# Transposes shared out anew between TensorE and DMA in a planned attention-and-experts kernel

## The chip, the cores and the metric

One core of one Trainium2 chip runs the whole program. The metric is the device time of one execution in microseconds (us). Three runs before the change took 315.46, 314.18 and 314.10 us; their median is 314.18.

## What is computed

The reference is an attention with soft-capped scores, whose output goes through four attention experts of which each token uses two. `B, H, S, Dh = 8, 12, 448, 64`; the model width `D` is 768, there are `E = 4` experts with one head of 64.

```python
scores = cap * tanh((q @ k.T) / sqrt(64) / cap)           # 8 x 12 heads of 448 x 448, cap = 30
x = softmax(scores) @ v                                    # heads side by side: 8 x 448 x 768
logits = x @ w_gate                                        # 4 experts, the best 2 of each token
w = softmax over the 2 chosen logits
for e in range(4):
    a = softmax(causal(x @ wq[e] @ (x @ wk[e]).T / 8))     # 448 x 448, each row sees its past
    out += (e chosen) * w * (a @ (x @ wv[e]) @ wo[e])
```

The soft cap bounds the first scores, so no row maximum is needed there.

## The kernel before

**Two stages, interleaved.** The work of the first stage goes by pairs of heads: 48 pairs, six for each batch (`HP = 6`). The last batch's pairs (42 to 47) hold only their first 320 queries (`W1`); the remaining 128 queries of its six pairs are packed into two more items, 48 and 49. For an item the keys of two heads are cast to 16 bits on GpSimd (POOL), turned by TensorE (PE) with four transposes (three of 128 keys, one for the 64-key tails of both heads), the query likewise, and one VectorE (DVE) copy brings both into `qk`. Scores are computed transposed (keys on partitions) into the banks `X` (three: the first key block of both heads, and the tails of both) and `Y` (two, used twice: `Y1`, `Y2`). ScalarE (ACT) applies tanh to X, Y1 and Y2 and then one exp to all seven slots of the item (lines L768 and L780). The value product gives outputs and, from a column of ones, the sums; DVE divides (L823, L826) into `xk`, PE turns `xk` (L841) and DVE copies it to `xT` (L850).

**Second stage, batch by batch.** When a batch's six pairs are done, `b_v` computes logits and values of all experts, POOL works out the gate (ranks, two one-hot masks `ms`, weights `mw`), `b_mask` widens each of the two masks to the 128 columns of a pair of experts (`mB`) and turns it by a DMA transpose into `mT`, `b_qk` computes keys and queries, and the query is multiplied with the turned mask as it leaves PSUM (`qm`, L951). So one score matmul handles four experts at once, each token with its own expert. `b_score` puts a slot's 1024 score columns into X0 and X1, ACT applies exp (L1066), POOL zeroes what lies ahead of the diagonal (L1076, L1083), `b_pv` makes the product with the values, `b_ot` adds the two slots on POOL (`oS`, L1141) and turns the sum by DMA into `oT`, and `b_wo` multiplies with `wo` and stores four windows of rows. The slots of batch b run beside pairs `6(b+1)+5` and `6(b+1)+6`, those of batch 6 beside items 48 and 49 (`exps`, L756). The last batch has no later pairs to hide behind: `last` and `last2` compute it by themselves at the end. There the causal mask is put into PSUM by matmuls with an identity (`negm`, L1290) before the scores are added.

**The order is planned.** Every operation is noted in a graph with the engine, an estimated duration and what it reads and writes. Exps and tanhs of ACT have a fixed order; they give due times, and `solve` (L130) plays the program through, engine by engine, taking the operation due first among those ready, with some seeded noise (`SEEDS`, `JIT`). Operations marked `first` go ahead of others when they come ready soon. The result is one order for each engine; on the chip each engine takes its instructions in that order and waits for what they need. DMA loads, stores and transposes are issued by SyncE (SP), also in the planned order. Three PSUM banks (`A0` to `A2`) serve everything but the scores while the pairs run; the five score banks are lent out only at the end.

**Lines that matter later.** `turned` (L387) issues a DMA transpose; `cast` (L615) the POOL casts (L620 keys, L635 key tails `ktz`, L639 values); `tr` (L647) the transposes of an item; `tr_first_tails` (L685) those of pair 0's tails, which are done apart; `fill` (L729) the score matmuls (L717 heads, L727 tails). `fill` groups an item's Y2 with the next item's X into one operation unless the item is in the set `alone` (L757), which holds the items that the second stage uses X0 and X1 beside. `normed` (L1189) ends the last batch's rows: division, transpose (L1208), the copy `oTL`, the product with `wo` (L1223), copies into `ob` and stores. The tiles `ob` are those into which `b_wo` writes as well. `evac` lets the planner choose DVE or ACT for a copy from PSUM, after ACT's fixed list is over (L377 in the profile, whatever engine).

## Time and profile before

| what | value |
|---|---|
| median of three runs | 314.18 us |
| the profiled execution | 314.04 us, of which 312.0 us from first to last instruction (the span) |
| mean granted TensorE clock | 0.983 |
| moved by DMA | 53.29 MB, 171 GB/s over the span |
| HBM read, written | 36.19 MB, 11.01 MB |
| instructions | 8950 |

The page of the profile gives busy time of each engine, the span in 40 slices, the chain of work that ended last, and the costliest groups of instructions by line of the kernel. Views of the trace give the same for any stretch: instructions in order of time with what ended the idle time before them ("[1.46 <-PE X L727]" is 1.46 us of idle time that ended when that matmul was done), busy time by stretch, waits by cause, DMA issues. In a busy-time row the engines stand as busy us and, in brackets, the number of instructions; then come the granted TensorE clock, the share of time in which the 16 DMA engines moved data, and GB/s. PE's matmuls are pipelined, so their durations overlap. In the 40 slices of 7.8 us the DMA share falls through the run:

```profile
DMA  6899999869976995789873698855014200531136
GB/s 183 182 227 221 297 272 253 220 168 268 251 189 159 313 272 159 187 179 255 217 164 78 201 310 196 129 162 154 2 41 146 97 2 19 87 120 60 36 148 207
```

### The profile page before, as it was taken

The numbers are of one execution on the slowest core, as the hardware profiler recorded it, in microseconds if no ns is written. First come the engines' busy times: TensorE is split into PE (matmuls) and PEld (weight loads), VectorE is DVE, ScalarE is ACT, GpSimd is POOL, SyncE is SP. The second block draws the span as 40 slices with busy tenths as digits, with TensorE's granted clock in tenths as the row PEclk, the third lists the DMA queues.
The fourth block names the chain that finished last, engine by engine and source line by source line (L and its number), as shares of the span: only waits on it lengthen the run. The fifth ranks groups of instructions, "written<-read, shape, count | busy, mean of one in ns | idle before, by whom it ended". The sixth has DMA issues, their size and how long they took to land.

```text
span 312.0 us, 8950 instructions
## 1 busy us (share of the span) xinstructions
PE 280.9 (90%) x3476; PEld 190.4 (61%) x3476; DVE 217.8 (70%) x645; ACT 291.8 (94%) x246; POOL 181.4 (58%) x498
## 2 busy tenths in 40 slices
PE   7677689979898899989998999999999989999993
PEld 3354356658564766657655776568664866667761
DVE  2345556666764886869766877788776877786883
ACT  4699999998999999999999999999999999999562
POOL 7694436996787452984785576947866414701200
PEclk9979979998999999999999999999999999999999
DMA  6899999869976995789873698855014200531136
GB/s 183 182 227 221 297 272 253 220 168 268 251 189 159 313 272 159 187 179 255 217 164 78 201 310 196 129 162 154 2 41 146 97 2 19 87 120 60 36 148 207
DMA packets 87482, 53.29 MB, mean 171 GB/s; under 512 B 48144, under 2 KB 83728, under 8 KB 87440
## 3 DMA queue, kind: packets, MB, share of 16 engines
q1 hardware_dynamic: 87136, 52.49, 65.5%
q8 instruction: 27, 0.44, 0.6%
q10 hardware_dynamic: 304, 0.23, 0.2%
q14 instruction: 15, 0.12, 0.2%
HBM read 36.19 MB, written 11.01 MB: 151 GB/s over the span
## 4 chain that ended last, share of the span: by engine, by line
ACT 66%; PE 20%; DMA 4%; POOL 3%; issue 3%; DVE 2%; SPq 1%; ACTq 0%; POOLq 0%
ACT yp L768 34%; ACT yp L780 28%; ACT pB L1066 4%; PE A L1164 2%; DMA kf<-in_k_dram 2%; PE Y L717 2%; PE A L937 2%; PE A L910 2%; PE A L802 2%; DMA out_dram<-ob 2%; PE X L1057 1%; PE A L1116 1%; PE A L663 1%; PE A L795 1%; PE X L727 1%
## 5 line engine op out<-in xcount | busy, mean ns | idle before, releaser
L780 ACT ACTIVATE yp<-yp 128x3136 f16<-128x3136 f16 (+4 forms) x51 | 139.0, 2726 | 0.0
L768 ACT ACTIVATE yp<-Y 128x896 f16<-128x896 f32 (+2 forms) x100 | 94.6, 946 | 2.6 <-PE Y L717 2.6
L768 ACT ACTIVATE yp<-X 128x1344 f16<-128x1344 f32 (+2 forms) x50 | 65.1, 1302 | 2.5 <-PE X L727 1.5
L802 PE MATMUL A<-v,yp 128*128 128x65 f16 x1116 | 56.4, 194 | 0.0
L802 PEld LDWEIGHTS <-yp 128*128 128x128 f16 x1116 | 49.0, 98 | 5.7 <-issue 2.9
L795 PE MATMUL A<-vtz,yp 128*128 128x130 f16 x186 | 41.3, 222 | 7.9 <-ACT yp L780 3.7
L826 DVE TENSOR_TENSOR xk<-A,rca 128x256 f16<-128x256 f32 (+1 forms) x96 | 39.7, 415 | 2.9
L717 PE MATMUL Y<-qk 64*128 64x448 f16 (+2 forms) x216 | 36.2, 341 | 5.7 <-ACT yp L768 5.1
L639 POOL CAST v<-vf 128x384 f16<-128x384 f32 x48 | 24.6, 514 | 27.0 <-PE A L802 22.1
L620 POOL CAST k<-kf 128x384 f16<-128x384 f32 x47 | 23.7, 513 | 24.2 <-PE A L663 15.0
L683 DVE COPY qk<-A 128x960 f16<-128x960 f16 x47 | 29.5, 650 | 6.1 <-PE A L653 6.0
L377 DVE COPY ob<-A 128x384 f32<-128x384 f32 (+1 forms) x56 | 30.4, 554 | 4.7 <-PE A L1164 2.9
L823 DVE RECIPROCAL rca<-A 128x4 f32<-128x4 f32 (+1 forms) x96 | 17.1, 178 | 21.0 <-PE A L802 19.4
L795 PEld LDWEIGHTS <-yp 128*128 128x128 f16 x186 | 18.1, 97 | 19.7 <-ACT yp L780 9.3
L623 POOL CAST q<-qf 112x512 f16<-112x512 f32 x44 | 27.2, 619 | 2.3 <-DMA qf<-in_q_dram 2.1
L717 PEld LDWEIGHTS <-qk 64*128 64x128 f16 x324 | 15.0, 93 | 21.7 <-issue 15.5
L1164 PE MATMUL A<-wo,oT 128*128 128x384 f16 x112 | 26.2, 326 | 1.4 <-DVE xT L850 0.5
L1131 DVE SCALAR_TENSOR_TENSOR oB<-A,rcb,mw 128x256 f16<-128x256 f32 x54 | 25.5, 481 | 1.8
L850 DVE COPY xT<-A 128x448 f16<-128x448 f16 (+1 forms) x48 | 18.0, 376 | 9.9 <-PE A L841 9.5
L1141 POOL TENSOR_TENSOR oS<-oB,oB 128x512 f16<-128x512 f16 x14 | 16.1, 1154 | 14.5 <-DVE oB L1131 8.7
L1116 PE MATMUL A<-vB,pB 128*128 128x260 f16 x133 | 22.2, 275 | 1.6 <-DVE oB L1131 1.2
L653 PE MATMUL A<-ident,q 112*128 112x112 f16 x192 | 22.5, 219 | 0.0
(210 smaller groups left out, 569.8 us busy)
## 6 DMA issues: line engine op xcount, KB each, us to landing
qf<-in_q_dram SPq DMA_DIRECT2D x23, 448.0 KB, 6.0
kf<-in_k_dram SPq DMA_DIRECT2D x23, 384.0 KB, 5.2
vf<-in_v_dram SPq DMA_DIRECT2D x23, 384.0 KB, 4.9
out_dram<-ob SPq DMA_DIRECT2D x23, 384.0 KB, 3.8
out_dram<-ob SPq DMA_DIRECT2D x9, 192.0 KB, 2.9
ktf<-in_k_dram SPq DMA_DIRECT2D x46, 32.0 KB, 4.9
vtf<-in_v_dram SPq DMA_DIRECT2D x46, 32.0 KB, 4.3
ob<-in_moe_wv_dram SPq DMA_DIRECT2D x2, 384.0 KB, 4.1
```

What stands on the lines that cost most here:

```text
L377: (nc.scalar.copy if o.eng == "ACT" else nc.vector.tensor_copy)(dst(), src())
L623: e(q16[i], qf[s][:, h].rearrange("p h (c d) -> p c h d", c=QC))
L683: lambda: nc.vector.tensor_copy(qk[t], bank16(g)[:, 0 : S + 512]),
L717: nc.tensor.matmul(dst[:, g, o], t[r, S + 128 * (c + 1) : S + 128 * (c + 2)], t[r, qs], start=True, stop=True,)
L768: ACTS[what, p] = act(c_act(n * (b - a)), lambda: nc.scalar.activation(y[:, a:b, 0:n], src[:, 0 : b - a, 0:n], AF.Tanh, scale=isc / capf), ...
L780: act(c_act(n * (b - a), False), lambda a=a, b=b, n=n: nc.scalar.activation(y[:, a:b, 0:n], y[:, a:b, 0:n], AF.Exp, scale=capf), ks, ks, f ...
L795: nc.tensor.matmul(ps[:, n, :, :], y[:, 2, w : w + 128], vtz[u], start=(n == 0), stop=False, skip_group_check=True,)
L802: nc.tensor.matmul(ps[:, n, h, :], y[:, SLOT[c][h], w : w + 128], v16[u][:, h, c, :], start=False, stop=(c == 2), skip_group_check=True,)
L826: dve(c_dve(128 * m), lambda g=g, i=i, rc=rc, m=m: nc.vector.tensor_tensor(xk[p % NXK][:, 2 * i : 2 * i + m, :, :], view(g)[:, 0:m, :, 0:D ...
L1116: nc.tensor.matmul(bank(g)[:, 0 : E * (Dh + 1)], pB[pi][:, o : o + 128], vB[x][:, c, :, :], start=(t == 0), stop=(t == len(cs) - 1),)
L1131: dve(c_dve(E * Dh) + 0.06, lambda g=g, k_=k_, n=n: nc.vector.scalar_tensor_tensor(oB[s][:, n, :, :], view(g)[:, :, 0:Dh], rcb[k_][:, 0, : ...
L1164: nc.tensor.matmul(bank(g)[:, 0 : D // 2], oT[x][n // 2][:, r, n % 2, :], wo2[r][:, c0:c1], start=(r == 0), stop=(r == 1),)
```

## The change

1. **Masks and outputs of batches 0 to 3** (`b < MD`, `MD = 4`). The masks `mB` are turned by TensorE: eight transposes a slot, and `qm` is now the product of a query kept in `qB` (a new copy from PSUM, two a batch) with the turned mask in PSUM. The query product no longer waits for the masks, and `b_qk` is noted after the gate. The slot sums `oS` are turned by eight TensorE transposes, with two copies to `oT`. Batches 4 to 6 keep the DMA transposes.
2. **Keys from pair 34 on** (`KD = 34`). Keys and tails of two pairs are cast by POOL into `kz` and turned by one DMA transpose of eight blocks into `kd` (three buffers of two pairs), from which the score matmuls read. TensorE turns only the query; the copy into `qk` is that of the query alone.
3. **x from pair 36 on** (`NAT = 36`). The query copy puts the queries into natural order, so `xk` needs no permutation and is turned by a DMA transpose straight into `xT`; the last pair of each batch (41 and 47) stays on TensorE. The value product then reads windows that run 64 columns past an item's last slot, into a pad.
4. **The last batch's causal masks** for the first 320 queries: the `negm` matmuls are gone; POOL zeroes the blocks after the exp. The masks of the last 128 queries (`neg2`) stay as they are.
5. **The start.** The key tails' cast is marked `first`, and POOL takes operations of that kind early (before 12 us of the plan). Item 0 is in `alone`, so its Y2 is filled without item 1's X. A wait for the first Y is dropped from pair 0's tail transpose. The first exp on ACT, which loads the table, waits for `ident` as well.
6. **The end.** Batch 6's first slot runs beside item 47 instead of 48. `b_wo` of batch 6 does three windows; its last 64 rows are put beside the 64 new rows of the last batch's third window by a POOL copy, and share its product with `wo`. `normed` writes its rows into the tiles `kf`, which held the keys, instead of `ob`, and has three tiles `oTL` instead of two.
7. **The planner's numbers**: estimates of DMA times, rank constants, due times, seeds. They change the order of instructions throughout.

The core of the diff:

```diff
-LAND = 2.2
+LAND = 1.95
-JIT = 0.784
-TWIRE = 0.2
-TOCC = 0.18
+JIT = 0.549
+TWIRE = 0.1
+HEAD = 12.0
+MD = 4
+NAT = 36
+KD = 34
...
-                if e in ("PE", "DVE") and not o.first:
+                early = e == "POOL" and t < HEAD
+                if (e in ("PE", "DVE") or early) and not o.first:
                     for t2, u in c:
-                        if u.first and u.due + lag < t + o.occ + 0.0 and t2 < t + max(SWITCH + 0.01, min(o.occ, 0.25)):
+                        if u.first and u.due + lag < t + o.occ + 0.04 and t2 < t + (
+                                o.occ if early else max(SWITCH + 0.01, min(o.occ, 0.25))):
...
+        def kcast(p):
+            s, o, x, j = p // 2 % NST, p % 2, p % (2 * NST), p // 2
+            dst = kz[j % 2][:, o]
+            gp(0.45, lambda: nc.gpsimd.tensor_copy(
+                dst[:, 128:].rearrange("p (c h d) -> p c h d", h=2, d=Dh),
+                kf[s][:, 2 * o : 2 * o + 2].rearrange("p h (c d) -> p c h d", c=KC)),
+                [("kf", x)], [("kz", j % 2, o, "k")], name=f"k16_{p}")
+            gp(0.2, lambda: nc.gpsimd.tensor_copy(
+                dst[:, 0:128], ktf[s][:, o].rearrange("p g d -> p (g d)")),
+                [("ktf", x, 0), ("ktf", x, 1), ("zk", s)], [("kz", j % 2, o, "t")],
+                name=f"kt16_{p}")
...
+        elif p % 2 == 0:
+            kcast(p)
+            kcast(p + 1)
+            j = p // 2
+            turned(8, lambda: kd[j % 3].rearrange("p o c -> p (o c)"),
+                   lambda: kz[j % 2].rearrange("p o c -> p (o c)"),
+                   [("kz", j % 2, o_, y) for o_ in range(2) for y in "kt"], [("kd", j % 3)],
+                   f"kT{p}")
...
-    exps = {HP * (b + 1) + (XOFF if b < LB - 1 else (6, 7))[s]: (b, s) for b in range(LB) for s in range(2)}
-    alone = set(exps)
+    late = {6: (5, 7)}
+    exps = {HP * (b + 1) + o: (b, s) for b in range(LB) for s, o in enumerate(late.get(b, XOFF))}
+    alone = {0, *exps}
...
+        if p >= NAT and p not in (PB - 1, NP - 1):
+            turned(nb, lambda: xT[b % 2][:, j, 0 : 128 * nb],
+                   lambda: xk[p % NXK][:, 0:nb].rearrange("p n g d -> p (n g d)"),
+                   [("xk", p % NXK, 0), ("xk", p % NXK, 1)], [("xT", b % 2, j)], f"xT{p}",
+                   due=due)
+            return
...
+                if b < MD:
+                    dve(c_dve(S), lambda g=g, r=r: nc.vector.tensor_copy(
+                        qB[x][r], bank(g)[:, 0:S]), [("q", b, r)], [("qB", x, r)], g, name=f"qB{b}")
+                    continue
...
+        if b < MD:
+            for r in range(2):
+                g = Group(AUX + XB, 1.3)
+
+                def mm(g=g, r=r):
+                    for n in range(4):
+                        nc.tensor.transpose(
+                            bank16(g)[:, 128 * n : 128 * (n + 1)],
+                            mB[s][:, r, n].rearrange("p e d -> p (e d)"), ident)
+
+                pe(0, mm, [("mB", s), "ident"], [("mt", b, s, r)], g, occ=0.22, name=f"mT{b}")
+                dve(c_dve(S, True), lambda g=g, r=r: nc.vector.tensor_tensor(
+                    qm[s][r], qB[x][r], bank16(g)[:, TL:512], ALU.mult),
+                    [("mt", b, s, r), ("qB", x, r)], [("qm", s, r)], g, name=f"qm{b}")
+            return
...
-        for n in range(4):
+        for n in range(4 if b < LB - 1 else 3):
...
-        o = ob[n]
+        o, u = kf[n].rearrange("p h x -> p (h x)"), n % 3
+        kk = [("kf", 2 * n), ("kf", 2 * n + 1)]
...
+        if n == 2:
+            y = (LB - 1) % 2
+            gp(0.25, lambda: nc.gpsimd.tensor_copy(oTL[u][:, :, 0:64], oT[y][:, 1, :, 1, 64:128]),
+               [("oT", y, 1)], [("oTL", u, 1)], name="oT6")
+            ko.append(("oTL", u, 1))
...
-            for e in (1, 0):
-                n = 128 if part == 0 else W1
-                pe(n, lambda e=e, n=n: nc.tensor.matmul(
-                    bank(g2[e])[:, 0:n], ident, negm[:, 0:n], start=True, stop=False,
-                    skip_group_check=True), ["negm", "ident", ("kB", x, r)],
-                    [("sL", r, part, e)], g2[e], name="mk")
+            pe(0, lambda: None, [("kB", x, r)], [("sL", r, part, 1)], g2[1], occ=0.0, name="op")
...
+            for o, base in ((64 + W1 * part, 0), (64 + W1 + 192, -64))[0 : 1 + part]:
+                def below(o=o, base=base):
+                    blk = pP[r][:, :, o : o + 128]
+                    nc.gpsimd.affine_select(
+                        out=blk, in_=blk, compare_op=ALU.is_ge, fill=0.0, base=base,
+                        pattern=[[0, 2], [1, 128]], channel_multiplier=-1)
+
+                gp(0.38, below, [], [("pB", pi, part) for pi in (2 * r, 2 * r + 1)], name="diagL")
...
-        o.first = o.name[:2] in ("sX", "sY", "sT", "tr", "qk", "k1", "q1", "ge")
+        o.first = o.name[:2] in ("sX", "sY", "sT", "tr", "qk", "k1", "q1", "ge", "kt")
```

177 lines of the change are left out of this document (111 added, 66 removed).

## Prediction

> **What bounds the kernel now.** I read the page's first part, then busy time by stretch, then what ScalarE (ACT) waited for.
>
> ```profile
> span 312.0 us, 8950 instructions
> PE 280.9 (90%) x3476; PEld 190.4 (61%) x3476; DVE 217.8 (70%) x645; ACT 291.8 (94%) x246; POOL 181.4 (58%) x498
> ```
>
> The profiled execution took 314.04 us, 2.04 more than its span; the median of the three runs is 314.18. I work on the span and add 2.04 at the end. ACT is busy for 94%. The stretches tell where the rest lies:
>
> ```profile
> core 0: us, PE busy (x) PEld busy (x) DVE busy (x) ACT busy (x) POOL busy (x), PEclk, DMA share, GB/s
> 0.00:12.51 12.51, 8.63 (x71) 4.68 (x72) 3.58 (x12) 5.61 (x8) 8.80 (x48) 1.00 0.81 196
> 12.51:66.00 53.49, 45.14 (x525) 28.11 (x525) 28.94 (x83) 53.49 (x39) 35.56 (x110) 0.94 0.96 237
> 66.00:190.00 124.00, 114.26 (x1442) 79.33 (x1442) 93.07 (x267) 122.84 (x93) 83.58 (x212) 0.99 0.80 208
> 190.00:276.00 86.00, 82.25 (x1032) 56.30 (x1030) 66.20 (x193) 85.99 (x71) 49.68 (x124) 1.00 0.39 92
> 276.00:290.04 14.04, 13.49 (x224) 10.81 (x220) 11.06 (x40) 13.38 (x13) 1.53 (x4) 1.00 0.29 100
> 290.04:312.00 21.96, 17.13 (x194) 11.17 (x189) 14.90 (x54) 10.51 (x27) 2.26 (x2) 0.99 0.42 139
> ```
>
> From 12.51 to 290.04 ACT runs almost without a break. That stretch is 277.53 us of tanh and exp, which the change doesn't touch. TensorE (PE) is nearly as full late in it: 82.25 of 86.00 us from 190 to 276. DMA goes the other way, from a share of 0.96 to 0.39. Two stretches are not ACT's: the first 12.51 us, with 5.61 of ACT work, and the last 21.96, with 10.51. ACT's waits by cause, within the stream:
>
> ```profile
> ACT yp L768 <- PE Y L717: 2.6, 2, 1.7
> ACT yp L768 <- PE X L727: 1.5, 1, 1.5
> ACT yp L768 <- PE X L717: 0.9, 1, 0.9
> ACT pB L1066 <- PE X L1057: 0.7, 1, 0.7
> ```
>
> The 1.5 and the longest of the first row (1.7) lie before 12.51. What can be had between 12.51 and 290.04 is the other two, 0.9 + 0.7 = 1.6 us, however much work moves there. So this is a change of the two ends; in the middle it can chiefly do harm.
>
> **The start.** The timeline of the first 13 us, with the issues of that stretch:
>
> ```profile
> 1.22 1.19 ACTq L481 DMA_DIRECT2D ktf<-in_k_dram  x2
> 6.23 0.92 ACT L768 ACTIVATE yp<-Y 128x896 f16<-128x896 f32 x1 [0.91 <-PE Y L717]
> 7.32 0.53 POOL L635 CAST ktz<-ktf 128x128 f16<-128x128 f32 x2
> 8.34 0.66 DVE L683 COPY qk<-A 128x960 f16<-128x960 f16 x1 [0.19 <-PE A L653]
> 8.61 1.29 ACT L768 ACTIVATE yp<-X 128x1344 f16<-128x1344 f32 x1 [1.46 <-PE X L727]
> 10.91 0.34 PE L663 MATMUL A<-ident,k 128*128 128x128 f16 x3 [1.66 <-POOL k L620]
> 11.59 0.92 ACT L768 ACTIVATE yp<-Y 128x896 f16<-128x896 f32 x1 [1.69 <-PE Y L717]
> 11.89 0.77 DVE L623 CAST q<-qf 112x512 f16<-112x512 f32 x2 [2.89 <-DMA qf<-in_q_dram]
> 17.07 0.93 ACT L768 ACTIVATE yp<-Y 128x896 f16<-128x896 f32 x1
> ktf<-in_k_dram ACTq DMA_DIRECT2D x2, 16.0 KB, 3.4
> ```
>
> Pair 0's X tanh waits 1.46 us for the scores of the key tails. Their cast stands at 7.32 on GpSimd (POOL), behind memsets, though the tails were issued from 1.22 on and landed 3.4 us later: the second, issued near 1.8, by about 5.3. From cast to tanh the trace needs 8.61 − 7.32 = 1.29 us. Cast at once, the scores stand at 5.3 + 1.29 = 6.6, before the Y tanh ends at 6.23 + 0.92 = 7.15. So the first wait, 1.46, goes.
>
> The second wait, 1.69, is an order: pair 0's second Y half is filled by one PE instruction group together with pair 1's X, and that stands behind the transposes of pair 2's keys, which start at 10.91 after waiting for a late load. With pair 0 in `alone` the Y half is filled for itself and needs only bank Y, free at 7.15. That wait goes too: 3.15 together.
>
> What is late next: pair 1's X needs its copy, which ends at 8.34 + 0.66 = 9.00; the new tanh would want it at 12.51 − 3.15 = 9.36, with 0.36 of matmul between: just met. Then pair 1's last Y is filled with pair 2's X, whose q is cast at 11.89 when it lands. Cast 0.4, transposes 0.4, copy 0.66 and two score matmuls 0.6, with hand-overs, end near 14.2; ACT would want it 3.15 before its present 17.07, at 13.9. I take **−2.8**; ends −1.2 (pair 2's q lands 1.6 late, as much as the keys made PE wait) and −3.15.
>
> **The middle.** What is moved:
>
> ```profile
> L841 PE MATMUL A<-perm,xk 128*128 128x128 f16 x144 | 16.3, 223 | 1.1 <-DVE xk L826 0.9
> L947 DVE CAST kB<-A 128x448 f16<-128x448 f32 x14 | 8.7, 624 | 8.1 <-PE A L937 7.9
> L850 DVE COPY xT<-A 128x448 f16<-128x448 f16 (+1 forms) x48 | 18.0, 376 | 9.9 <-PE A L841 9.5
> L389 SPq DMA_TRANSPOSE mT<-mB x14: 1232/1258/2520, 60.1 to 269.4; - x14
> mT<-mB SPq DMA_TRANSPOSE x14, 2.8
> SPq L389 <- POOL oS L1141: 41.4, 5, 14.0
> 202.23 0.63 DVE L683 COPY qk<-A 128x960 f16<-128x960 f16 x1
> 215.03 1.29 ACT L768 ACTIVATE yp<-X 128x1344 f16<-128x1344 f32 x1
> ```
>
> A 128 by 128 transpose occupies PE for 16.3 / 144 = 0.113 us. Batches 0 to 3 gain 16 for the masks and 8 for the outputs each: 24 × 0.113 = 2.7 us a batch, 10.9 in all, before about 190 us. VectorE (DVE) gains per batch two q evacuations like `kB` (0.62) and two output copies (about 0.38): 2.0 us, 8.0 in all. Off PE come four key transposes for each of 14 pairs (34 to 47) and 35 x transposes (five pairs of four, five of three): 91 × 0.113 = 10.3 us, nearly all after 190. DVE loses ten x copies, 3.8 us; its key and query copy shrinks.
>
> Early there is room: PE idles 8.35 us from 12.51 to 66 and 9.74 from 66 to 190, DVE 24.6 and 30.9. With 18 us of idle for 10.9 of new work, and ACT never idle beside it, I cost this at nothing; without that cover up to half of 2.7 us a batch would stand before the batch's scores.
>
> On SP eight mask and eight output transposes of about 1.25 us leave; seven key transposes (two pairs, eight blocks each) and ten x transposes come. A key transpose is issued in 1.26 us and lands 2.8 after its issue, and waits for POOL casts that exist now. It has time: the copy of pair 36's keys starts at 202.23 and their tanh at 215.03, 12.8 us of lead. Last pairs of a batch keep TensorE, so x's DMA latency isn't on a batch's path. The new waits stand in SP's queue, ahead of stores and the last loads; those lead by whole pairs. The Trainium skill (VectorE: DVE Perf Modes, "The three transpose paths") gives 390 ns a block on TensorE and 1309 ns by DMA and prefers TensorE where PSUM can take the result; by it, an estimate, a key transpose would take 10.5 us and seven of them 73. The trace disagrees, with 2.8 us for the same eight blocks. I take **0** for the middle; ends −1.6 (both waits gone) and +3 (half of 2.7 us in two batches).
>
> **The end.** After the stream:
>
> ```profile
> 289.16 0.88 ACT L780 ACTIVATE yp<-yp 128x768 f16<-128x768 f16 x1
> 290.00:300.00 10.00, 10.00 (x117) 7.03 (x114) 7.94 (x33) 5.62 (x17) 2.26 (x2) 1.00 0.12 28
> 290.04:312.00 21.96, 1.26 (x8) 0.61 (x8) 0.99 0.42 139
> 290.04:312.00 21.96, 1.91 (x10) 0.85 (x10) 0.99 0.42 139
> 290.04:312.00 21.96, 3.39 (x16) 1.37 (x16) 0.99 0.42 139
> 305.58 0.48 ACT L377 COPY ob<-A 128x384 f32<-128x384 f32 x1 [1.09 <-DMA out_dram<-ob]
> 306.98 0.37 ACT L377 COPY oTL<-A 128x256 f16<-128x256 f16 x1
> 308.27 0.48 ACT L377 COPY ob<-A 128x384 f32<-128x384 f32 x1 [0.92 <-PE A L1223]
> L567 POOL TENSOR_SCALAR_AFFINE_SELECT negm<-negm 128x128 f16<-128x128 f16 x2 | 0.6, 294 | 0.1
> ```
>
> The first stretch row is of all engines up to 300; the other three are those of the mask matmuls (L1290), of the last batch's q and k (L1247) and of batch 6's output projection (L1164) alone. PE is busy 17.13 of 21.96 us here, and its last matmul ends just before the copy at 308.27: this stage is PE's backlog with a chain of evacuations at its end.
>
> 1. The eight mask matmuls go: −1.26. Six selects on POOL come, each on two heads' blocks (0.29 each, as L567 shows for one block, to twice that). POOL has 2.26 us of work here, so they cost only latency between exp and value product. I take zero, at most +0.5.
> 2. Batch 6's last window joins the last batch's third: a quarter of 3.39 goes, −0.85; two evacuations of about 0.5 go from DVE and ACT, and a small POOL copy comes.
> 3. PE has 10.3 us less to do before the stream ends and batch 6's first expert slot runs a pair earlier, so q and k of the last batch can be done before the stream ends. Of the 1.91 us that now lie behind it I take −1.7.
> 4. Output rows go to the idle `kf` tiles: ACT's 1.09 wait for a store of `ob` goes. Part of it hid behind PE: the row at 306.98 could start near 306.6. I take −0.4.
>
> Sum **−4.2**. Ends: −1.0 (only the mask matmuls, less their selects' latency) and −6.5 (the v products move ahead too).
>
> **Sum:** 312.0 − 2.8 + 0 − 4.2 = 305.0; plus 2.04, **307.0 us**.
>
> **Rivals.**
>
> A. Only the start pays: at the end a chain of evacuations, not PE, sets the time, so lighter PE work buys only idle time. For: PE idles 4.8 us there already. Against: up to 300 it isn't idle at all (10.00 of 10.00). 311.2 us, 0.15.
>
> B. The new transposes of batches 0 to 3 crowd PE and its three spare PSUM banks, so a batch's scores come late: half of 2.7 us in each of four batches is +5.4, less 7.0: 312.4 us. Against: idle PE time. 0.10.
>
> C. **Slower:** keys by DMA come late. SP works in order and has waited up to 14.0 us for POOL's `oS` before an output transpose. A key transpose behind such a wait lands 14.0 + 1.3 + 2.8 = 18.1 us after its cast. It decides from the point where this passes the lead, 12.8 us: 5.3 us of ACT idle. Batch 4's output transposes and stores fall among the key transposes, and ten x transposes add waits of their own; three hits, less what falls in slack, cost about 12, against −7.0: 319 us, 0.10. The skill's 1309 ns a block would lead to the same place.
>
> D. The moved work changes nothing that ends last and the new order loses what the start gains: 314 us, 0.05.
>
> **How the numbers follow.** The forecast's own case, 0.60, spans 303.5 to 310.5. About 0.5% (1.6 us) is what a measurement of this kernel tells from no change. Faster: 0.60 + 0.15 + 0.06 of B = 0.81; same, the rest of B and D: 0.09; slower: 0.10. The range that leaves out C, D and a little: 303.5 to 313.
>
> **What would show it.** Start: pair 0's three tanh without a wait over 0.2 us, the third ending near 9.4; a wait at a later Y for pair 2 would be the smaller end. Middle: from there to the last exp of the stream 277.5 us ± 1.5, with no ACT wait on a score that waited for `kd`. End: from the last exp to the span's end 17.8 us instead of 21.96, no L1247 matmul behind the stream and no ACT wait on a store. Wrong if ACT waits appear at pairs 34 to 49 released by DMA, or if the end keeps its 22 us.

## The result and the profile after

The changed kernel takes 315.43 us (median of 20 runs, 312.72 to 318.33), the kernel before 313.35 us beside it (20 runs, 311.48 to 315.46). The ratio is 1.0058, with a 95% interval of 1.0033 to 1.0083: 0.6% slower, where 307.0 us and "faster" were forecast. Every ratio and interval in this text leaves out the runs that took over 1.5% more than the fastest of their kernel (three of the changed kernel's 20), while the medians are of all runs.

The first part of the page of the changed kernel answers to the two lines that the prediction begins with:

```profile
span 312.4 us, 8949 instructions
PE 282.7 (90%) x3469; PEld 188.7 (60%) x3469; DVE 215.2 (69%) x649; ACT 291.9 (93%) x246; POOL 182.7 (58%) x506
```

The profiled execution took 314.15 us, 1.3 less than the median of its kernel; what it lost is less than what a usual execution loses. Busy time by stretch, up to pair 0's exp, then as before to 66, 190, 276, the end of the stream's last exp and the span's end:

```profile
core 0: us, PE busy (x) PEld busy (x) DVE busy (x) ACT busy (x) POOL busy (x), PEclk, DMA share, GB/s
0.00:12.14 12.14, 9.68 (x75) 5.00 (x75) 2.85 (x10) 7.28 (x10) 8.58 (x43) 1.00 0.71 188
12.14:66.00 53.86, 45.97 (x523) 28.31 (x522) 30.03 (x86) 52.38 (x39) 30.69 (x105) 0.90 0.93 234
66.00:190.00 124.00, 117.35 (x1509) 80.80 (x1506) 93.39 (x272) 121.69 (x93) 89.01 (x230) 1.00 0.76 200
190.00:276.00 86.00, 79.72 (x956) 52.94 (x955) 63.10 (x187) 85.07 (x69) 48.03 (x117) 1.00 0.42 100
276.00:292.13 16.13, 15.08 (x239) 11.63 (x239) 12.62 (x45) 15.24 (x15) 1.69 (x5) 1.00 0.36 110
292.13:312.40 20.27, 14.89 (x177) 10.06 (x175) 13.23 (x51) 10.28 (x27) 4.66 (x9) 1.00 0.44 151
```

The first of these bounds isn't that of the rows before, which was the end of the third tanh; pair 0's exp began at 14.37 there and begins at 12.14 here. The work moved as the prediction said: TensorE is busier from 66 to 190 (117.35 against 114.26) and freer after (79.72 against 82.25). The last stretch shrank from 21.96 to 20.27. But the last exp of the stream ends at 292.13, 2.09 later than before, although the start is earlier.

A mark that both kernels have is the end of pair 1's exp: 22.69 before, 19.45 + 2.81 = 22.26 after. From there to the end of the stream's last exp it is 290.04 − 22.69 = **267.35** before and **269.87** after. So in this execution the start gives 0.43, the middle takes 2.52, the end gives 1.69: +0.4 on the span, where 7.0 less were forecast. ACT's waits by cause from 12 to 292 show the middle's loss:

```profile
ACT yp L819 <- PE Y L766: 3.3, 5, 1.2
ACT pP L1143 <- PE X L1134: 1.4, 2, 0.9
```

With two rows of 0.3 and 0.2 that is 5.2 us, of which 1.48 lie before 22; before, the same causes cost 1.6 in all after 12.51. The other 3.7 are 1.17 + 0.50 at pairs 22 and 23, 0.25 + 0.18 at pair 28, 0.76 at pair 40 and 0.89 for batch 6's scores. The two longest, by ACT's timeline:

```profile
139.57 0.92 ACT L819 ACTIVATE yp<-Y 128x896 f16<-128x896 f32 x1 [1.17 <-PE Y L766]
277.95 1.02 ACT L1143 ACTIVATE pP<-X 128x1024 f16<-128x1024 f32 x1 [0.89 <-PE X L1134]
```

The start, by ACT's timeline:

```profile
7.32 0.92 ACT L819 ACTIVATE yp<-Y 128x896 f16<-128x896 f32 x1 [1.65 <-PE Y L766]
...
9.30 0.93 ACT L819 ACTIVATE yp<-Y 128x896 f16<-128x896 f32 x1
...
15.16 0.92 ACT L819 ACTIVATE yp<-Y 128x896 f16<-128x896 f32 x1 [0.20 <-PE Y L766]
16.39 1.29 ACT L819 ACTIVATE yp<-X 128x1344 f16<-128x1344 f32 x1 [0.32 <-PE X L776]
18.64 0.92 ACT L819 ACTIVATE yp<-Y 128x896 f16<-128x896 f32 x1 [0.96 <-PE Y L766]
```

The two waits of pair 0 are gone, and the third tanh ends at 9.30 + 0.93 = 10.23 instead of 12.51, though the first begins 1.09 later than before. Then pairs 1 and 2 give most of it back: 0.20 + 0.32 + 0.96.

### The profile page after: what moved, and what is told of

It reads as the page before. It is cut to its first block, busy times and chain, and to the rows that moved or that the text cites. A ratio compares the mean times of both kernels' runs of the same rounds, so it can differ in the third digit from the quotient of the medians.

```text
span 312.4 us, 8949 instructions
## 1 busy us (share of the span) xinstructions
PE 282.7 (90%) x3469; PEld 188.7 (60%) x3469; DVE 215.2 (69%) x649; ACT 291.9 (93%) x246; POOL 182.7 (58%) x506
## 4 chain that ended last, share of the span: by engine, by line
PE 32%; ACT 29%; POOL 18%; DMA 10%; DVE 6%; issue 4%; ACTq 0%; DVEq 0%; POOLq 0%
ACT yp L819 15%; ACT yp L831 12%; DMA kd<-kz 4%; PE A L995 4%; PE Y L766 3%; PE A L854 3%; POOL mB L1090 3%; PE A L968 2%; PE A L1255 2%; ACT pP L1143 2%; PE X L1134 2%; DMA vf<-in_v_dram 2%; PE A L1193 2%; PE A L846 2%; POOL k L630 1%
## 5 line engine op out<-in xcount | busy, mean ns | idle before, releaser
L819 ACT ACTIVATE yp<-Y 128x896 f16<-128x896 f32 (+2 forms) x100 | 96.4, 964 | 5.0 <-PE Y L766 5.0
L729 DVE COPY qk<-A 128x960 f16<-128x960 f16 x33 | 21.2, 652 | 10.9 <-PE A L685 10.7
L1255 PE MATMUL A<-wo,oT 128*128 128x384 f16 x108 | 24.6, 326 | 4.5 <-DVE ob L382 2.2
L382 DVE COPY ob<-A 128x384 f32<-128x384 f32 (+1 forms) x49 | 26.0, 553 | 3.4 <-PE A L1255 1.7
L766 PE MATMUL Y<-qk 64*128 64x448 f16 x136 | 25.3, 366 | 0.7 <-ACT yp L819 0.4
L1193 PE MATMUL A<-vB,pP 128*128 128x260 f16 x134 | 21.9, 274 | 1.7 <-DVE oB L1208 1.7
L630 POOL CAST k<-kf 128x384 f16<-128x384 f32 x33 | 16.6, 516 | 11.3 <-DMA kf<-in_k_dram 6.7
L968 PE MATMUL A<-wvg,xT 128*128 128x260 f16 x168 | 22.6, 274 | 0.2
L995 PE MATMUL A<-xT,wk 128*128 128x448 f16 x84 | 21.9, 353 | 0.7 <-DVE oB L1208 0.5
L685 PE MATMUL A<-ident,q 112*128 112x112 f16 x192 | 20.9, 213 | 1.4 <-DVE ob L382 0.5
```

Of the source, the lines that this page charges most:

```text
L382: (nc.scalar.copy if o.eng == "ACT" else nc.vector.tensor_copy)(dst(), src())
L766: nc.tensor.matmul(dst[:, g, o], kT[r, 128 * (c + 1) : 128 * (c + 2)], t[r, qs], start=True, stop=True,)
L819: ACTS[what, p] = act(c_act(n * (b - a)), lambda: nc.scalar.activation(y[:, a:b, 0:n], src[:, 0 : b - a, 0:n], AF.Tanh, scale=isc / capf), ...
L968: nc.tensor.matmul(bank(g)[:, 0 : E * Dh + E], xT[x][:, j, w : w + 128], wvg[:, j, :], start=(j == 0), stop=(j == NDC - 1),)
L995: nc.tensor.matmul(bank(g)[:, o : o + t.stop - t.start], w2[:, j, :], xT[x][:, j, t], start=(j == 0 and o == 0), stop=(j == NDC - 1), skip ...
L1193: nc.tensor.matmul(bank(g)[:, 0 : E * (Dh + 1)], pB[pi][:, o : o + 128], vB[x][:, c, :, :], start=(t == 0), stop=(t == len(cs) - 1),)
```

## Theories and experiments

**Theory.** The middle loses because GpSimd works in order and has new casts in its queue that wait for DMAs. A cast into one of the two `kz` buffers waits until the last key transpose out of that buffer (`kd<-kz`) has landed, and for its own load of `kf`; behind it in the written order stand a batch's gate (L1035 to L1069), masks (L1090) and the next pairs' casts. What is late there reaches ACT several pairs on. The waits by cause of GpSimd from 150 to 176, after:

```profile
POOL kz L639 <- DMA kd<-kz: 2.3, 3, 1.1
POOL kz L635 <- DMA kf<-in_k_dram: 0.9, 1, 0.9
```

and before, where nothing on GpSimd waits for a DMA in that stretch (the two longest of four rows, all for PE or DVE):

```profile
POOL v L639 <- PE A L802: 3.4, 1, 3.4
POOL mw L1019 <- DVE g_w L1016: 1.4, 1, 1.4
```

**Rivals.** One: the new TensorE work of batches 0 to 3 crowds TensorE (rival B of the prediction). Two: the keys by DMA come too late at the score matmuls (rival C). Three: the change itself is sound, and it is its written order that loses.

A second cause, at pair 22, was seen in the trace of after. VectorE's and GpSimd's timelines beside each other:

```profile
131.86 1.70 DVE L1077 TENSOR_SCALAR g_w<-g_e 128x4 f32<-128x4 f32 x1 [0.28 <-POOL g_e L1069]
```

```profile
131.79 0.51 POOL L630 CAST k<-kf 128x384 f16<-128x384 f32 x1
132.23 0.61 POOL L645 CAST q<-qf 112x512 f16<-112x512 f32 x1
132.79 0.29 POOL L666 CAST ktz<-ktf 128x128 f16<-128x128 f32 x1
133.03 0.51 POOL L671 CAST v<-vf 128x384 f16<-128x384 f32 x1
```

An add of 128 by 4 numbers takes 1.70 us: it ends at 133.56, when the fourth of four back-to-back casts ends (133.54). What is queued behind it on VectorE is late, and the 1.17 at 139.57 follows; gw_pool, below, tries whether it does so for that reason.

In the experiments the planner's list of after is kept and single entries are moved in it, by lines of this form behind the planner's call; the numbers are those of the operations in the list:

```diff
     order = G.solve(when, AUX, XB + YB)
+    for x, ref in MOVES:          # x goes directly behind ref
+        order.remove(G.ops[x])
+        order.insert(order.index(G.ops[ref]) + 1, G.ops[x])
```

Besides single executions there is one measure by which all are compared: the end of pair 1's exp, the stretch from there to the last exp of the stream, and from there to the span's end.

| kernel | pair 1's exp ends | middle | end | median of runs (n) |
|---|---|---|---|---|
| before | 22.69 | 267.35 | 21.96 | 313.35 (20) |
| before_again | 22.56 | 267.11 | 22.13 | 313.78 (1) |
| after | 22.26 | 269.87 | 20.27 | 315.43 (20) |
| start_trt | 21.42 | 271.23 | 20.35 | 314.73 (12) |
| start_all | 20.36 | 270.38 | 20.26 | 312.95 (12) |
| kz3 | 21.62 | 270.80 | 20.28 | 313.15 (12) |
| gw_pool | 21.71 | 272.66 | 20.23 | 316.57 (12) |
| gw_first | 21.13 | 272.33 | 20.24 | 315.44 (12) |
| keys_late | 20.64 | 268.18 | 20.38 | 311.73 (12) |
| mask_back | 20.21 | 271.66 | 21.43 | 314.73 (12) |
| best | 20.26 | 267.02 | 20.32 | 310.24 (6) |
| best_nostart | 21.36 | 266.45 | 20.29 | 310.00 (6) |
| seeds0 | 20.93 | 268.32 | 21.45 | 312.82 (12) |
| before_seeds0 | 23.33 | 273.19 | 24.48 | 321.00 (6) |
| seeds0_md0 | 20.20 | 278.57 | 20.93 | 322.18 (6) |
| seeds0_kd48 | 20.62 | 271.50 | 21.88 | 317.22 (6) |

The first three columns are of one profiled execution each. The kernels were run in several groups; the kernel before ran again beside each, with medians from 312.97 to 313.31.

### start_trt and start_all: the start's order

```diff
+MOVES = [(78, 73), (79, 74)]                       # start_trt: pair 0's tails behind its q
+MOVES = [(78, 73), (79, 74), (136, 7), (168, 136), # start_all: also tails of pairs 2, 3 cast early,
+         (70, 168), (162, 175), (178, 162)]        # pair 2's Y scores ahead of pair 0's value product
```

> The changed kernel in its own written order, but pair 0's transpose of the key tails stands behind its query transposes on TensorE, and the copy of the tails behind the query copy on VectorE. Theory (the first tanh is late because of this place in the order, but what comes next is bound by the casts of pair 2's and 3's key tails on GpSimd): the first tanh starts at 6.2 us instead of 7.32, the second pair's last Y tanh still near 15.1, so the exp of pair 1 ends at 22.1 to 22.3 (22.26 in the changed kernel): time of the whole -0.2 to 0. Rival (the first tanh sets the start): everything behind it moves by 1.1 us, the exp of pair 1 ends at 21.2, whole -1.1. The order from 25 us on is that of the changed kernel, so the waits near 139, 143, 246 and 278 us should come again within 0.2 us if they belong to the order, and not if they were an accident of the one profile.

> As the run with the tails' transpose moved, and besides: GpSimd casts the key tails of pairs 2 and 3 ahead of two groups of memsets, and the first Y scores of pair 2 stand ahead of pair 0's value product on TensorE. Theory: the tails are cast near 12.8 instead of 13.9, pair 1's last Y tanh starts near 14.1 instead of 15.16, the wait of 0.96 before the Y tanh at 18.64 goes, and the exp of pair 1 ends at 19.9 to 20.4 instead of 22.26; the gain of about 2.1 us holds to pair 10 at least, whole -2. Rival (loads bound the start, so that the lead is lost at the next late load): the exp of pair 1 ends early but the lead is under 0.5 us by pair 10.

In start_trt the first tanh began at 7.62, no earlier than in after (7.32); q's transposes began at 5.87, when q had landed, and the PSUM bank that they write became free with ACT's copy at 5.68. So what set the first tanh here is the landing of q, and not the tails' transpose; the bank was free 0.19 earlier, and in best, which exchanges the banks, the first tanh still began at 7.06. Neither side's number was met. Pair 1's exp ended at 21.42, and 314.73 us is 1.0025 [0.9996, 1.0054] of before. Of the waits that were to come again within 0.2, those at 139 and 143 did (1.17 and 0.50) and so did the one at 278 (1.07 for 0.89); the one at 246 was 0.40 for 0.76, and pair 28's grew from 0.25 to 1.44. So the first three belong to the order, and the other two change with the execution.

In start_all the start does what was expected of it: from 14.75 on pair 1 runs without a wait and ends at 20.36. The middle keeps its loss (270.38), and the whole takes 312.95 us, 0.9999 [0.9972, 1.0026]. The later kernels whose start was left as in after ended pair 1 at 20.21 (mask_back), 20.64 (keys_late), 21.13, 21.36, 21.62 and 21.71, by themselves: 22.26 was the latest of seven. Their mean is 21.28, against 22.63 in two profiles of before. So the change's start is worth about 1.35, with 2 us of scatter between executions, and the moves of start_all buy nothing that can be told from it (best against best_nostart, below). Why the median of start_all is 2.5 below that of after all the same wasn't followed up; it warns against reading a difference of that size between two of these medians as the price of one move.

### kz3: three buffers instead of two

```diff
-    kz = [sb(f"kz{i}", [128, 2, 512]) for i in range(2)]
+    kz = [sb(f"kz{i}", [128, 2, 512]) for i in range(3)]   # and j % 3 at both uses
```

> The changed kernel in its own written order with three instead of two buffers for the key casts that go into the DMA transposes. Theory (a key transpose that lands 4.7 us after its issue holds the buffer, so GpSimd's next key cast waits 1.23 us at 229.6, and batch 5's masks behind it come late): the wait of 1.23 us on GpSimd goes, the mask transposes of batch 5 are issued 1 to 1.2 us earlier, and ScalarE's waits of 0.76 and 0.11 near 246 and 250 us shrink to under 0.2: whole -0.7 to -1.1. Rival (TensorE and VectorE are full there, so the stall comes from them): GpSimd's wait goes but ScalarE's stays over 0.5, whole 0.

GpSimd's timeline ahead of batch 5's gate, after:

```profile
229.56 0.50 POOL L635 CAST kz<-kf 128x384 f16<-128x384 f32 x1 [1.23 <-DMA kd<-kz]
230.03 0.38 POOL L1036 TENSOR_SCALAR g_d<-g_c 128x64 f32<-128x64 f32 x1
```

and kz3:

```profile
228.60 0.51 POOL L635 CAST kz<-kf 128x384 f16<-128x384 f32 x1
229.07 0.39 POOL L1036 TENSOR_SCALAR g_d<-g_c 128x64 f32<-128x64 f32 x1
```

A gate step at 230.03 stood behind a cast that had waited 1.23 for a transpose; with a third buffer it doesn't wait. Counted from the gate's first step (L1035), the masks come 1.28 earlier, and ACT's 0.76 wait at 246.16 falls to 0.46: only a part, since TensorE waits there for `oT` too. GpSimd then waited 1.64 for a load of `kf` elsewhere. So the cause is real, but not alone. What it is worth in time isn't shown: the median is 313.15, 2.3 below after, but start_all, which leaves these casts alone, is as far below, and the middle of kz3's profile is no shorter (270.80).

### gw_pool and gw_first: the add of pair 22

```diff
...
-        dve(0.11, lambda: V.tensor_scalar_add(w0, e, 1.0), ...
+        dve(0.11, lambda: nc.gpsimd.tensor_scalar_add(w0, e, 1.0), ...
+MOVES = [(410, 404), (703, 697), (1033, 1027), (1363, 1357),   # gw_first only: the add
+         (1689, 1688), (2013, 2012), (2329, 2328)]             # directly behind its power
```

> The changed kernel in its own written order, with the addition of 1 to the second gate weight (128x4, once a batch) on GpSimd instead of VectorE. Theory (VectorE's form of it waits while GpSimd casts without a break: 1.70 us at 131.86, and the evacuation, TensorE and the Y scores behind it are late): the stalls of 1.17 and 0.50 us near 139 and 143 go, the exp of pair 22 ends 1.1 to 1.6 earlier counted from pair 21, whole -1.2 to -1.6. Rival (TensorE's new transposes in batches 0 to 3 crowd it, and the VectorE wait only chose the place): ScalarE still waits 0.8 us or more in total between 131 and 146.

> As the run with the gate weight's addition on GpSimd, but the addition stands directly behind the power in GpSimd's queue instead of up to three casts later. Theory: the gain at pairs 22 and 23 (1.7 us) stays, and VectorE no longer waits 4.2 us at 171; pair 28's stall is that of the changed kernel, 0.3 to 1.2 us; median 1 to 2 us below the changed kernel. Rival (the stall of 5.15 us at pair 28 has nothing to do with the place of the addition): pair 28 loses 3 us or more again.

Pair 22 gained 1.28 as expected: its exps stand 5.47 apart at 132.76 and 138.23, with no wait between. So the add does cause the loss at pair 22. The whole didn't follow: gw_pool's runs spread from 311.09 to 319.36, wider than any other's, and its ratio to before, 0.9982 [0.9938, 1.0026], doesn't tell it from before. Its profiled execution is one of the long ones (316.74) and loses at pair 28. By its timelines, on GpSimd:

```profile
160.06 0.29 POOL L639 CAST kz<-ktf 128x128 f16<-128x128 f32 x1 [1.72 <-DMA kd<-kz]
...
167.69 0.50 POOL L635 CAST kz<-kf 128x384 f16<-128x384 f32 x1 [0.50 <-DMA kf<-in_k_dram]
168.16 1.05 POOL L1069 TENSOR_TENSOR g_e<-eul,g_e 128x4 f32<-128x4 f32 x1
169.16 0.51 POOL L630 CAST k<-kf 128x384 f16<-128x384 f32 x1
...
170.65 0.24 POOL L1077 TENSOR_SCALAR g_w<-g_e 128x4 f32<-128x4 f32 x1
```

then VectorE, TensorE and ACT, each in its own timeline:

```profile
170.92 0.18 DVE L1078 RECIPROCAL g_w<-g_w 128x4 f32<-128x4 f32 x1 [4.24 <-POOL g_w L1077]
```

```profile
171.68 0.27 PE L846 MATMUL A<-vtz,yp 128*128 128x130 f16 x1 [3.81 <-DVE xk L878]
```

```profile
172.80 0.92 ACT L819 ACTIVATE yp<-Y 128x896 f16<-128x896 f32 x1 [2.04 <-PE Y L766]
...
178.14 0.92 ACT L819 ACTIVATE yp<-Y 128x896 f16<-128x896 f32 x1 [3.23 <-PE Y L766]
```

This is the chain of the theory, whole: a key cast waits for DMA (3.1 us for `kf` and 1.7 for `kd<-kz` between 150 and 170), the gate behind it is late, VectorE stands 4.24 for the gate, TensorE 3.81 for VectorE's `xk`, and ACT 2.04 and then 3.23. The two ACT waits are together longer than the 3.81 of TensorE, and the stretches of gw_pool suggest why:

```profile
167.00:171.00 4.00, 0.87 (x16) 0.59 (x13) 0.08 (x1) 3.76 (x3) 3.50 (x8) 0.99 0.05 14
171.00:174.40 3.40, 2.72 (x26) 1.77 (x25) 2.30 (x10) 1.60 (x2) 3.34 (x10) 0.50 0.40 77
174.40:177.60 3.20, 3.20 (x38) 3.13 (x36) 2.53 (x8) 0.50 (x1) 1.52 (x6) 0.50 0.69 181
```

After the idle stretch the granted clock (the column behind POOL's) is 0.50 for 6.6 us, to 177.60, and TensorE works without a break in the second half of that; behind 178.5 the clock is 1.00 again. The Trainium skill (TensorE: Matmul & The Clock Gate, "Part 1: The HAM clock gate") says that the throttled state is the default and that activity releases it; the trace agrees, with 0.50 behind 3.81 us of idling.

In gw_pool the add itself stands three casts behind its power (168.16 and 170.65), so it could have been the add's place. gw_first puts it directly behind, and pair 28 lost again: ACT waited 3.37 and 0.71, GpSimd 3.9 for `kd<-kz` and 2.1 for `kf` between 150 and 176, and the median is 315.44. VectorE's wait for the gate fell from 4.24 to 1.89 and TensorE's for `xk` from 3.81 to 1.47, so the add's place had a share in those; but the loss remained, with the waiting key casts, and the clock halved here too:

```profile
174.00:176.00 2.00, 2.00 (x23) 1.40 (x21) 1.00 (x3) 0.06 (x1) 0.37 (x2) 0.50 0.68 185
```

Where the add is still VectorE's, its own wait for the gate step ahead of it can be set beside ACT's wait at pair 28. The shortest and the longest, after and start_trt:

```profile
169.12 0.46 DVE L1077 TENSOR_SCALAR g_w<-g_e 128x4 f32<-128x4 f32 x1 [0.52 <-POOL g_e L1069]
```

```profile
169.81 0.46 DVE L1077 TENSOR_SCALAR g_w<-g_e 128x4 f32<-128x4 f32 x1 [1.72 <-POOL g_e L1069]
```

In after, start_all, mask_back, kz3 and start_trt VectorE waits 0.52, 0.63, 0.79, 1.35 and 1.72 there, and ACT then 0.25, 0.36, 0.52, 1.09 and 1.44: each time 0.27 or 0.28 less. What the gate is late by reaches ACT one for one, and the granted clock stays at 1.00 in all five. Both profiles with 4 us and more at this pair have the clock at 0.50 behind it.

### keys_late: the key casts behind the gates

```diff
+MOVES = [(1861, 1537), (2065, 1747), (2066, 2065), (2068, 2066), (2431, 2068), (2432, 2431),
+         (2123, 2122), (2125, 2123), (2436, 2386), (2438, 2436), (2437, 2438), (2439, 2437)]
```

These are casts of keys or key tails of pairs 36, 38 to 41, 46 and 47, put behind the gates of batches 3 and 5, and the two loads of pair 46's key tails, which need their buffers. Nothing else is changed.

> The changed kernel in its own written order, but GpSimd's casts of the keys of pairs 36, 38 to 41, 46 and 47 (with two loads that need their buffers) stand behind the gate of batch 3, and of batch 5, instead of ahead of it and among it; nothing needs these keys before 200 us. Theory (what moves the time from one execution to the next is GpSimd's queue: key casts that wait for a DMA hold the gate of the batch behind them, VectorE waits for the gate and TensorE for VectorE): no wait on kd<-kz or kf on GpSimd between 150 and 170 us ahead of the gate, the exp of pair 28 ends 5.5 to 5.6 us after that of pair 27 (5.86 in the changed kernel, 7.06, 6.7, 10.65 and 5.97 in four variants of it), ScalarE's waits near 246 and 250 us together under 0.3 us (0.87), the median 1 to 1.7 us lower and the highest run under 317 (318.33). Rival (TensorE is too full there, GpSimd only shows it): pair 28 and pair 40 keep their stalls.

GpSimd's waits by cause from 152 to 168, keys_late:

```profile
POOL oS L1218 <- DVE lg L977: 2.4, 1, 2.4
```

No wait for a DMA is left ahead of the gate, pair 28's exp ends 5.50 behind pair 27's, the stream's own pace, and ACT has no wait between the 0.50 at 142.07 and 274. The middle is 268.18, and the median 311.73: 3.7 below after, more than the 1 to 1.7 that were expected, with a highest run of 314.72 against 318.33. The profile of after shows only 0.25 + 0.18 of loss at pair 28, that of start_trt, with the same order there, 1.44, those of gw_pool and gw_first 2.04 + 3.23 and 3.37 + 0.71. The loss there changes from execution to execution, and one profile is a poor measure of it. That the place of these casts costs time is shown: the waits go with it, and by the ratios to before, 0.9976 [0.9949, 1.0003] against after's 1.0058, it is 0.8%, 2.6 us. How much of the medians' 3.7 is theirs isn't, nor that every long execution of after loses it at pair 28.

### mask_back: the end's mask matmuls alone

```diff
...
+                m = 128 if part == 0 else W1
+                for e in (1, 0):
+                    nc.tensor.matmul(bank(g2[e])[:, 0:m], ident, negm[:, 0:m], start=True,
+                                     stop=False, skip_group_check=True)
...
-                gp(0.38, below, [], ...                       # the selects
+                gp(0.38, lambda: None, [], ...
```

> The changed kernel in its own written order with the last batch's mask matmuls back ahead of its scores on TensorE and without the six selects on GpSimd. Theory (behind the stream the stage is TensorE's backlog): it lasts 1.0 to 1.3 us longer than the 20.27 of the changed kernel, about the 1.26 us of the matmuls. Rival (a chain of evacuations and selects sets it): under 0.4 longer, or shorter, since the selects' 0.41 to 1.48 us leave the chain from exp to value product.

The last stretch:

```profile
291.87:313.30 21.43, 15.98 (x186) 10.65 (x183) 13.28 (x51) 10.59 (x27) 2.43 (x3) 0.99 0.42 143
```

TensorE is busy 15.98 instead of 14.89, and the stage takes 21.43 instead of 20.27: +1.09 and +1.16. The end is TensorE's backlog, one for one, and the selects on GpSimd (4.66 against 2.43 busy) cost nothing that shows. Rival A of the prediction falls with this. The median, 314.73, isn't above that of after; the 1.16 us are read from one profile each.

### best and best_nostart: the repairs together

best has the moves of start_all (q's transposes ahead of the tails' by exchanging their PSUM banks), gw_first and keys_late, and one more: batch 6's mask transpose ahead of a transpose of x in SP's queue. best_nostart is the same without the start's moves.

```diff
+MOVES += [(2293, 2291)]      # mT of batch 6 ahead of an xT on SP
```

> All moves together in the changed kernel's order: pair 0's query transposes ahead of the tails' and in another bank, the tails of pairs 2 and 3 cast ahead of memsets, pair 2's Y scores ahead of pair 0's value product, the key casts behind the gates of batches 3 and 5, the gate weight's addition on GpSimd behind the power, and batch 6's second mask transpose ahead of an x transpose on SP. Theory (single waits in four queues, not the amount of work, cost the change its gain): first tanh near 6.3 us, pair 10 at least 1.25 us earlier, pair 22 1.7, pair 28 0.4 or more, pairs 40 and 47 0.9 each: 308 to 310.5 us against the 315.4 of the changed kernel and the 313.3 of the kernel before. Rival (full engines: each wait that is taken away comes back at the next place): not under 312.5.

> As the run with all moves together, without those of the first 20 us. Theory (the start is bound by what lands when, and the moves there buy little): within 0.7 us of the 310.24 of all moves. Rival (the order of the start costs what the first comparison of the profiles showed, 1.9 us): 311.5 to 312.5.

SP's issues and the query product that needs them, after:

```profile
269.82 1.21 SPq L394 DMA_TRANSPOSE xT<-xk  x1
271.12 1.26 SPq L394 DMA_TRANSPOSE mT<-mB  x1
```

```profile
275.47 0.62 DVE L1013 TENSOR_TENSOR qm<-A,mT 128x448 f16<-128x448 f32 x1 [1.22 <-DMA mT<-mB]
```

and best's SP, where both stand ahead of the x transpose:

```profile
264.39 2.58 SPq L394 DMA_TRANSPOSE mT<-mB  x2
```

With that, ACT's waits by cause in best, from 12 to 287.2, are

```profile
ACT yp L819 <- PE Y L766: 0.6, 2, 0.4
ACT yp L819 <- PE X L766: 0.4, 1, 0.4
```

and 0.2 for `pP`, 1.2 us instead of 5.2. The first tanh stayed at 7.06, against the 6.3 that was hoped for. best takes 310.24 us, **0.9918 [0.9890, 0.9946]** of before; best_nostart 310.00, 0.9919 [0.9895, 0.9943]. Both beat both kernels, by at least 3.1 and 5.2 us, and only the order is changed from after, with an add on another engine (and in best two PSUM banks exchanged). The start's moves are worth nothing.

### before_again: the same kernel once more

> The kernel before once more, for a second profile. Six profiles in which the changed kernel's order is the same up to 20 us end pair 1's exp anywhere from 20.2 to 22.3 us. Theory (loads land differently from one execution to the next, in both kernels): here it ends 0.3 us or more from the 22.69 of the first profile, while the stretch from there to the last exp of the stream stays 267.4 within 0.7. Rival (only the changed kernel scatters, before is the same each time): both within 0.2.

It changes nothing; it is a second profile of before. Pair 1's exp ended at 22.56 and the middle took 267.11: by these marks two executions of before agree within 0.25, while seven with after's start spread over 2.05. That is the rival's side, on two executions.

### The order apart from the change

Both orders are a planner's, with due times shifted by a list of numbers (`SEEDS`). With all of them zero, neither order is chosen by its shifts, though each kernel keeps the rest of its planner's numbers:

```diff
-SEEDS = (0, 471, 650, 88, ...
+SEEDS = (0,) * 78
```

> The changed kernel planned anew with all of the SEEDS at zero, so with the due times unperturbed; all else as in the changed kernel. Theory (the written order is worth several microseconds by itself, since single waits in the queues decide): the time is 2 to 10 us from 315.4, more likely longer. Rival (amount and kind of work decide, an order is as good as another): within 1 us of 315.4.

> The kernel before planned anew with all of its SEEDS at zero. With the same run of the changed kernel it shows what the change is worth when neither order has been chosen by its perturbations. Theory (the change takes 1.3 us of mask matmuls and more off TensorE, but puts waits into GpSimd's queue that the planner does not foresee): both lose 2 to 10 us against their own order, and the changed one loses at least as much. Rival (the change is good and only its chosen order was unlucky): the changed kernel is 2 us or more faster here.

after takes 312.82 us without its own list, 2.6 *less* than with it, where more had been thought likelier; before takes 321.00, 8.0 more, so the rival of before_seeds0 is what came. Between these two plans the change gains 321.00 − 312.82 = **8.2 us**. This is one plan of each kernel, and the shifts alone move the kernel before by 8.0, so it isn't the price of the change whatever the order. ACT's longest waits by cause within the stream, before_seeds0 and then seeds0:

```profile
ACT pB L1066 <- PE X L1057: 7.5, 4, 2.5
```

```profile
ACT pP L1143 <- PE X L1134: 2.0, 2, 1.5
```

The 7.5 are four waits for a batch's scores: 2.51, 2.13 and 1.73 for batches 0 to 2, and 1.08 at 286.71. In seeds0 the first three are gone; its 2.0 stand at 211.59 and 275.06, with batches whose masks still go by DMA. So this part of the gain lies where the masks were moved. Two parts were undone alone, on the plan without shifts:

```diff
-MD = 4
+MD = 0            # seeds0_md0: all masks and outputs by DMA
-NAT = 36
-KD = 34
+NAT = 48          # seeds0_kd48: all keys and x on TensorE
+KD = 48
```

> The changed kernel planned anew with all SEEDS at zero and MD at 0, so that masks and outputs of batches 0 to 3 are turned by DMA as in the kernel before. Theory (the masks on TensorE are what the change gains: the kernel before with unperturbed due times waited 2.51, 2.13 and 1.73 us for the scores of batches 0 to 2): waits of 1.5 us or more come back at two of these batches, the time is 316 to 319 against 312.8 with MD at 4. Rival (the key and x transposes by DMA and the new end are the gain): within 1.5 us of 312.8.

> The changed kernel planned anew with all SEEDS at zero, KD and NAT at 48: keys and x of every pair are turned on TensorE as in the kernel before, masks of batches 0 to 3 too. Theory (10.3 us of transposes come back to TensorE after 190 us, where it is nearly full, and the end gets its backlog): the stretch from 190 us and the end are 1.5 to 4 us longer, the time 314 to 317 against 312.8. Rival (TensorE had room, and the waits that the key casts put into GpSimd's queue go): 312 or less.

Without the masks on TensorE it takes 322.18 us, 9.4 more; ACT waits 6.9 for batches' scores, 3.07 of it for batch 6's, whose masks are the same in both, and 5.2 for Y, of which 2.49 and 1.51 follow a wait of 2.48 of VectorE's `qm` for one `mT`. Without keys and x by DMA it takes 317.22, 4.4 more; a single 4.0 wait for batch 6's scores stands at 277.93. Both gains are in the middle: 278.57 and 271.50 against 268.32. On this plan each is more than the 1.6 us that the prediction held to be in the middle at all. Both are above the ranges expected (316 to 319, 314 to 317). They needn't add up, and each changes the planner's whole order, so one plan of each gives the direction and not a price.

## Why the prediction was wrong

In the profile the three terms missed by nearly the same: the start by 2.37, the middle by 2.52, the end by 2.51, together the 7.4 us by which the span of 312.4 is above 305.0. The start and the end went the way that was forecast and were sized too large; the middle went the other way.

**The step that failed is the middle at 0.** It cost +2.5 us in the profile and +3.5 in the mean of after, start_trt, start_all and mask_back (270.8 against 267.2 in two profiles of before). The working reasoned that the idle time of TensorE and VectorE covers the new work, and that "it has time": the keys lead their tanh by 12.8 us. Both held, and neither was the question. It named SP's queue for the new waits and left out GpSimd's: of the step that moves the keys, it counted the seven transposes that are issued, but not that their casts now wait for a buffer that a transpose must have left, on the engine that also computes the gate. The key transposes landed a median 3.6 us after issue, not 2.8:

```profile
kd<-kz SPq DMA_TRANSPOSE x7, 3.6
```

Putting those casts behind the gate gave back 3.7 us of the median, 2.6 by the ratios. In the one profile of after they are the smaller part, 0.43 and 0.76 of the 3.7 us of waits behind 22. The larger parts are the add behind four casts (1.67), an accident of the order, and 0.89 in SP's queue after all, where a mask transpose stands behind one of the new x transposes, ahead of a batch's scores and not of a store.

**The written order was taken as neutral.** Item 7 of the change says that the order changes throughout; the sum had no term for it. By the medians it loses 2.6 us to a plan without shifts, and all repairs together give 5.4 (315.43 − 310.00), which needs no other code than the order and one add's engine. The 1.6 us "that can be had" in the middle was right for before's chosen order only.

**The start** was forecast at −2.8 and came to −1.35 in the mean, −0.43 in the profile, nearer its smaller end of −1.2. Both waits of pair 0 went, as the prediction said, and the third tanh ended at 10.23, not 9.4, since the first began 1.09 later. "A wait at a later Y for pair 2 would be the smaller end": that is what came, 0.96 at 18.64, and in start_all it is gone, with 0.43 left a pair later.

**The end** was forecast at −4.2 and is −1.69. Of its terms, the mask matmuls are right: 1.1 measured alone, 1.26 forecast, and the selects at nothing are right. The store wait is gone. Batch 6's last window gave 0.48 of its 0.85 (L1255 is busy 2.91, before 3.39). The term that failed is the −1.7 for the last batch's q and k: 1.66 us of them (9 of 10) still lie behind the stream,

```profile
292.13:312.40 20.27, 1.66 (x9) 0.84 (x9) 1.00 0.44 151
```

because TensorE is busy 15.08 of the 16.13 us before 292.13: the work that left it had left earlier, from 190 to 276, where TensorE now idles 6.3 us, 3.75 before. ACT's longest wait behind the stream, 1.7, is for those matmuls. The "10.3 us less to do" on which the term rested were too many as well: from 190 to the span's end TensorE is busy 109.69 us, before 112.87, only 3.2 less, and that includes the mask matmuls. The stream is 0.8 us later at 190 than before, so a little other work lies there too; why so little was freed isn't shown. Without the mask matmuls the rest of the end gave about 0.5 (mask_back's 21.43 against 21.96).

**The rivals.** A (evacuations set the end) is refuted by mask_back. B (TensorE crowded in batches 0 to 3) is refuted: the repairs left the masks on TensorE, and ACT's waits went from 5.2 us to 1.2. C had the mechanism nearly right (an in-order queue in which something waits for the new DMAs ahead of a batch's work) and the wrong queue, place and price: GpSimd's, not SP's; the gate, not the keys' own scores; about 3 us, not 12. D (the order loses what the start gains, 314 us at 0.05) was the nearest in number, and it is the better summary: the change gains at the start and at the end, on the plans without shifts in the middle too, and its written order gives away more.

**Open.** Why the loss at pair 28 varies from execution to execution, 0.4 to 1.4 us in five profiles with the add on VectorE, 4 to 5 in two with it on GpSimd: it follows the lateness of the gate, and the loads and transposes that GpSimd waits for land at different times, but what makes them late was not tried. Nor was it tried what those two would lose with the clock at 1.00. The same holds for the 2 us of scatter of the start. Why the order of seeds0 avoids the waits was read only from its GpSimd rows, where none from 150 to 176 is for a DMA.

## What to carry to other kernels

When work is moved to DMA, list what the *producers* of its inputs now wait for, and what else stands behind them in their engine's queue: a cast that must wait for a buffer holds up the gate behind it, far from the data it casts. Where a kernel's order has been chosen among many, a structural change and its new order are two changes; price them apart, by running both kernels with several orders that were not chosen, before judging the structure (here it was one of each). A loss that depends on when transfers land is read from medians of many runs, since one profile can show 0.4 us of a loss that is 1.4 in another of the same order.

## What was not expected of the hardware

**A small VectorE operation can be held for a whole run of GpSimd casts.** The add at L1077 (128 by 4, fp32) took 0.16 us at its shortest, 0.46 in the median of its seven places, at most 0.70 in before, and 1.70 beside four casts in a row, in six of six profiles with that order. The Trainium skill (SBUF — State Buffer, "SBUF: two separate sides") calls the port pair that VectorE and GpSimd share an exclusive lock, held for the whole instruction by whichever starts first, where VectorE's operation runs in a two-port mode or has two inputs in SBUF. The trace agrees that something holds the add beside GpSimd, but by that rule, if the add falls under it, it would have waited for one cast, at most 0.61; it ended with the fourth. Whether the ports are the cause no run here shows; the runs show only the durations.

**The granted clock halved behind two stalls.** In gw_pool 3.81 us of idle TensorE were followed by 6.6 us at 0.50, and ACT's two waits behind them, 2.04 and 3.23, are together longer than the stall. In gw_first it was 1.47 us of idle time, to 169.17, with the clock at 1.00 up to 171 and at 0.50 from there to 177; VectorE had waited 1.89 for the gate, and ACT lost 3.37 and 0.71. In the five profiles where the clock stayed at 1.00 at this place ACT lost less than VectorE had waited. That the clock makes the difference is argued from these rows, since the two with the halved clock also have the add on GpSimd.
